# Loads of q and k issued behind GpSimd's regroup, and stores of x one iteration later, in an attention and mixture-of-experts kernel

## The chip, the cores and the metric

The kernel runs on one core of one Trainium2 chip. The core has a matrix engine (PE; PEld is its weight load), a vector engine (DVE), a scalar engine (ACT), GpSimd (POOL) and SyncE (SP), which issues most of the DMAs. All DMAs of the core share 16 DMA engines. The metric is the device time of one execution in microseconds.

## The reference

Attention in chunks of 64 keys, then an expert layer in which every token goes to one of eight experts, then a dense layer with a squared ReLU. All in float32.

```python
# q, k, v: (8, 8, 576, 64); chunk = 64
scores = scale * np.matmul(q_c, k_c.transpose(0, 1, 2, 4, 3))
attn = softmax(scores);  out = np.matmul(attn, v_c)
x = out.transpose(0, 2, 1, 3).reshape(4608, 512)
logits = x @ w_gate;  expert_idx = argmax(logits, axis=1)
out[mask] = gate_w[mask, None] * (np.maximum(x[mask] @ w1[e], 0.0) @ w2[e])   # for each of 8 experts
h = np.maximum(x @ w_in, 0.0);  return h * h @ w_out
```

## The kernel before

Three stages follow each other: `attention()` (0 to about 190 us), `experts()` and `second()`. Only the first is touched, and only it is described here.

**Tiles and units.** The 4608 tokens make 36 tiles of 128 (`NTILE`) and 18 units of two tiles. `load_qk(u)` brings q and k of a unit into one of four buffers (tag `a`), one DMA of 512 KB for each where the unit lies in one batch, two smaller ones where it crosses into the next. So a unit is 1.05 MB. v comes by batches (eight, 1.18 MB each, eight DMAs of 144 KB) from GpSimd's queue, into two buffers. x, the result of a tile, is 0.26 MB; it goes from one of four buffers (tag `x`) to `x_d` in HBM by SP, and PE transposes it from the same buffer for the gate.

**The loop** runs over `it` from -3 to 36. Iteration `it` holds, in this order: GpSimd's regroup of a few halves of units, `scores(it+1)`, `pv(it-1)`, `attn_t(it)`, the transposes of q and k that are four or five halves ahead, the transpose of an older tile's x, and every fourth iteration pieces of the gate: the logits (`gate`), the routing (`gate_t`, `route`), the places (`place`) and GpSimd's scatters of them. In this document tile t stands for what `pv(t)` computes in iteration t+1.

**Halves.** A half z is q (even) or k (odd) of unit z/2. `regroup(z)` (L269) copies it on GpSimd from the unit's buffer into one of four slots of `by_r`; `trans` (L296) transposes it on PE. Unit 0 is transposed straight from its buffer (L279).

**What sets the order.** The program order of each engine is the order in which the code is written. SP's queue holds the loads of q and k (L250), the stores of x (L359) and, from iteration 22, the first loads of the experts' weights (L172). A load of q and k waits until GpSimd has regrouped the unit that held the buffer before; a store waits for DVE's x (L358). What stands behind a waiting instruction on SP waits with it. `load_qk(u+3)` is issued where the last transpose of unit u is written; the store where `pv` has written x. In `pv`, DVE writes x (L358) into a buffer that is free when the store of four tiles before has landed and PE has transposed it; `pv` has one PSUM buffer, so the next tile's `pv` on PE waits for that write.

Of the kernel before, what the change touches and what calls it, by code (L numbers as in the profile page):

```python
# [20 lines left out]
def kernel(ctx, tc, q, k, v, w_gate, w1, w2, w_in, w_out, out):  # L21
    nc = tc.nc
# [7 lines left out]
    NTILE = NT // 128  # L30
    NUNIT = NT // 256
# [31 lines left out]
    x_d = dram.tile([NT, DM], F32, name="x_d")  # L63
# [11 lines left out]
    def tl(tag, shape, dt, name):  # L75
        if tag in fixed:
            ts, n = fixed[tag]
            fixed[tag] = ts, n + 1
            t = ts[n % len(ts)].bitcast(dt)
            k = 1  # L80
            for z in shape[1:]:
                k *= z
            t = t[0:shape[0], 0:k]
            names = "abcde"[:len(shape) - 1]
            return t.rearrange(f"p ({' '.join(names)}) -> p {' '.join(names)}", **dict(zip(names, shape[1:])))
        if tag == "m":

            t = sb.tile([128, 32], F32, tag=tag, name=name, bufs=NBUF[tag]).bitcast(dt)
            names = "abc"[:len(shape) - 1]
            n = 1  # L90
            for z in shape[1:]:
                n *= z
            return t[0:shape[0], 0:n].rearrange(f"p ({' '.join(names)}) -> p {' '.join(names)}", **dict(zip(names, shape[1:])))
        return sb.tile(shape, dt, tag=tag, name=name, bufs=NBUF[tag])
# [134 lines left out]
    def attention():  # L229
        with ExitStack() as actx:  # L230
# [8 lines left out]
            st = {}  # L239

            def load_qk(u):
                qk = tl("a", [128, 2, H, 2 * D], F32, f"qk{u}")
                for j, (src, nm) in enumerate(((q, "q"), (k, "k"))):
                    t = qk[:, j]
                    g = 4 * u
                    done = 0
                    while done < 4:
                        b, c = divmod(g + done, NCB)
                        n = min(4 - done, NCB - c)
                        nc.sync.dma_start(  # L250
                            out=t[32 * done:32 * (done + n)],
                            in_=src[b, :, c * CH:(c + n) * CH, :].rearrange("h (p r) d -> p h (r d)", r=2),
                        )
                        done += n
                    st[nm, u] = t
# [9 lines left out]
            def regroup(z):  # L265
                u, j = divmod(z, 2)
                if u:
                    src = st["qk"[j], u].rearrange("p h (r d) -> p r h d", r=2)
                    nc.gpsimd.tensor_copy(out=by_r[:, z % 4], in_=src)  # L269
# [36 lines left out]
            def scores(i):  # L306
                u, h2 = divmod(i, 2)
                qt, kt = st["qT", u], kb[u % 2]
                ps = ps_s.tile([128, H, CH], F32, tag="s", name="sc")
                for p in range(NPAIR):  # L310
                    for c2 in range(2):
                        c = 2 * h2 + c2
                        nc.tensor.matmul(
                            ps[64 * c2:64 * c2 + 64, 2 * p:2 * p + 2, :],
                            lhsT=qt[:, p, 32 * c:32 * c + 32, :].rearrange("p i r -> p (i r)"),
                            rhs=kt[:, p, c],
                            start=True,
                            stop=True,
                        )
                mx = tl("m", [128, H], F32, "mx")  # L320
                nc.vector.tensor_reduce(mx, ps, axis=AX.X, op=ALU.max)
                at = tl("r", [128, H, CH], F32, "at")
                nc.vector.tensor_tensor(out=at, in0=ps, in1=mx[:, :, None].to_broadcast([128, H, CH]), op=ALU.subtract)
                st["at", i] = at
# [5 lines left out]
            def attn_t(i):  # L330
                at = st.pop(("at", i))
                ps = ps_t.tile([128, NPAIR, 128], F32, tag="t", name="ta")
                for p in range(NPAIR):
                    nc.tensor.transpose(ps[:, p, :], at[:, 2 * p:2 * p + 2, :], ident)
                aT = tl("r", [128, NPAIR, 128], F32, "aT")
                nc.scalar.copy(aT, ps)
                st["aT", i] = aT

            def pv(i):
                aT = st.pop(("aT", i))  # L340
                ps = ps_v.tile([128, 2, 512], F32, tag="v", name="pv")
                for p in range(NPAIR):
                    for c2 in range(2):
                        b, c = divmod(2 * i + c2, NCB)
                        o = (p % 2) * 2 * (D + 1)
                        nc.tensor.matmul(
                            ps[64 * c2:64 * c2 + 64, p // 2, o:o + 2 * (D + 1)],
                            lhsT=aT[:, p, 64 * c2:64 * c2 + 64],
                            rhs=vb[b % 2][p][:, c].rearrange("p j d -> p (j d)"),
                            start=True,  # L350
                            stop=True,
                        )
                pv_ = ps[:, :, 0:4 * (D + 1)].rearrange("p a (h d) -> p a h d", d=D + 1)
                rc = tl("m", [128, 2, 4, 1], F32, "rc")
                nc.vector.tensor_scalar(out=rc, in0=pv_[:, :, :, D:D + 1], scalar1=1e-9, scalar2=None, op0=ALU.add)
                nc.vector.reciprocal(out=rc, in_=rc)
                x = tl("x", [128, 2, 4, D], F32, "x")
                nc.vector.tensor_tensor(out=x, in0=pv_[:, :, :, 0:D], in1=rc.to_broadcast([128, 2, 4, D]), op=ALU.mult)  # L358
                nc.sync.dma_start(out=x_d[128 * i:128 * i + 128, :], in_=x.rearrange("p a h d -> p (a h d)"))  # L359
                st["x", i] = x  # L360

            def get(shape, name):
                return ps_t.tile(shape, F32, tag="t", name=name)
# [39 lines left out]
            def fill_v(s, eng, ps):  # L403
                for t in vb[s][ps]:
                    eng.memset(t[0:64, :, 1, :], 0.0)
                    eng.memset(t[64:128, :, 0, :], 0.0)
                    eng.memset(t[0:64, :, 0, D:D + 1], 1.0)
                    eng.memset(t[64:128, :, 1, D:D + 1], 1.0)
# [37 lines left out]
            regrouped, moved = [0], [0]  # L446

            def trans_upto(z, hh):
                for y in range(moved[0], min(z, NTILE)):
                    u, h2 = divmod(y, 2)  # L450
                    trans("qk"[h2], u, hh)
                    if hh and h2 and u + 3 < NUNIT:
                        load_qk(u + 3)

            for it in range(-3, NTILE + 1):
                ahead_ = it + 4 + (it >= JUMP)
                while regrouped[0] < min(ahead_ + 2, NTILE):
                    regroup(regrouped[0])
                    regrouped[0] += 1
                if it in (-2, 0):  # L460
                    fill_v(1, nc.gpsimd, A if it < 0 else Z)
                if it in (-1, 0):
                    load_v(1, ps=HA if it < 0 else HZ)
                if 0 <= it + 1 < NTILE:
                    scores(it + 1)
                if 0 <= it - 1 < NTILE:
                    pv(it - 1)
                    lo, hi = (2 * (it - 1)) // NCB, (2 * (it - 1) + 2) // NCB
                    if hi > lo and lo + 2 < B:
                        load_v(lo + 2)  # L470
                if 0 <= it < NTILE:
                    attn_t(it)
                if it == JUMP:
                    for hh in range(2):
                        trans_upto(ahead_ - 1, hh)
                    moved[0] = ahead_ - 1
                trans_upto(ahead_, 0)
                for step, i in todo.get(it, ()):
                    step(i, nc.scalar.copy if any(f == gate_route for f, _ in late.get(it, ())) else nc.vector.tensor_copy)
                if 0 <= it + 1 < NTILE:  # L480
                    expo(it + 1)
                trans_upto(ahead_, 1)
                moved[0] = min(ahead_, NTILE)
                if it == 2:
                    constants()
                late_steps(it)
                if it == NTILE - 14:
                    for _ in range(4):
                        load_next(most=1)
                if NTILE - 5 <= it < NTILE - 2:  # L490
                    split(1, 0, it - NTILE + 5, eng=nc.gpsimd)
# [633 lines left out]
```

## Time and profile before

| | |
|---|---|
| median of 3 runs | 1461.23 us (1460.78 to 1465.03) |
| profiled execution, its own time | 1460.37 us |
| its span, first to last instruction | 1458.5 us |
| mean granted TensorE clock | 0.993 |
| PE busy | 1419.3 us, 97% of the span |
| POOL busy | 505.6 us, 35% |

How to read it: PE is busy nearly throughout, so what counts is the time in which it isn't, and the time in which its granted clock is below full. The page's slices are 36 us wide; attention is the first five of them. There PE shows 7 to 9 tenths, GpSimd 5 to 7 and DMA 9 in the first four. From the sixth slice on DMA falls below the full digit and PE stays at 8 and 9.

### The profile page before, as it was taken

How to read it: one execution, taken by the hardware profiler on the slowest of the kernel's cores; microseconds unless marked ns; L12 is line 12 of the kernel's file. 1: busy time of each engine (PE TensorE's matmuls, PEld its weight loads, DVE VectorE, ACT ScalarE, POOL GpSimd, SP SyncE). 2: the span in 40 equal slices, each digit the busy share in tenths (PEclk: the TensorE clock that was granted, in tenths of full speed). 3: DMA queues.
4: the chain of work that ended last, by engine and by line, in shares of the span. 5: the costliest groups of instructions: out<-in, count | busy, mean ns of one | idle time of the engine just before them, and what ended most of it. 6: DMA issues, size and time to landing. Idle time of an engine off the chain costs nothing.

```text
span 1458.5 us, 21568 instructions
## 1 busy us (share of the span) xinstructions
PE 1419.3 (97%) x8186; PEld 1222.9 (84%) x8186; DVE 761.5 (52%) x1371; ACT 549.6 (38%) x936; POOL 505.6 (35%) x608
## 2 busy tenths in 40 slices
PE   7988988999999999999999999999999999999998
PEld 5877788888889999997888888888888888888886
DVE  7767787578888788884432322322332232233222
ACT  4765634444444455554422222222222222222222
POOL 7675755436555446643003040210404012040301
PEclk9999999999999999999999999999999999999999
DMA  9999555767678778885101010100101001010000
GB/s 204 260 259 244 148 162 182 221 192 234 208 225 247 223 234 266 268 257 163 58 15 46 1 60 0 44 17 1 60 0 60 0 26 35 1 60 0 31 2 29
DMA packets 144369, 172.90 MB, mean 119 GB/s; under 512 B 18160, under 2 KB 103872, under 8 KB 144256
## 3 DMA queue, kind: packets, MB, share of 16 engines
q1 hardware_dynamic: 110032, 112.58, 27.0%
q0 software_dynamic: 17920, 40.51, 10.0%
q10 hardware_dynamic: 16304, 18.36, 3.8%
q8 instruction: 65, 1.06, 0.3%
q14 instruction: 48, 0.39, 0.1%
HBM read 133.05 MB, written 38.34 MB: 118 GB/s over the span
## 4 chain that ended last, share of the span: by engine, by line
PE 54%; POOL 0%; POOLq 0%; issue 0%; DVE 0%
PE hp L1034 27%; PE py L1055 27%; POOL out_dram L1015 0%; POOLq L1120 0%; DVE o L1063 0%; POOL between L1014 0%
## 5 line engine op out<-in xcount | busy, mean ns | idle before, releaser
L1034 PE MATMUL hp<-xm,w_None 128*128 128x512 f32 x1728 | 417.5, 391 | 3.3 <-DVEq L978 3.3
L1034 PEld LDWEIGHTS hp<-xm,w_None 128*128 128x128 f32 x1728 | 326.3, 189 | 71.5 <-ACTq L978 3.5
L1055 PE MATMUL py<-w_None,h 128*128 128x512 f32 x1512 | 363.2, 389 | 0.0
L1055 PEld LDWEIGHTS py<-w_None,h 128*128 128x128 f32 x1512 | 283.8, 188 | 58.8
L1039 DVE SCALAR_TENSOR_TENSOR rs<-hp,rs 128x512 f32<-128x512 f32 x144 | 99.5, 691 | 437.7 <-ACT rs L1038 437.7
L1038 ACT ACTIVATE rs<-hp 128x512 f32<-128x512 f32 x144 | 86.0, 597 | 460.0 <-PE hp L1034 460.0
L1015 POOL DMA_INDIRECT out_dram<-o,tp x36 | 35.1, 974 | 630.2 <-ACT o L1061 624.2
L796 PE MATMUL pa<-xs,w 128*128 128x256 f32 (+2 forms) x1344 | 242.3, 329 | 5.7 <-DVE h L800 2.4
L808 PE MATMUL pb<-h,w 128*128 128x256 f32 (+2 forms) x1344 | 243.9, 331 | 0.0
L796 PEld LDWEIGHTS pa<-xs,w 128*128 128x128 f32 x1344 | 211.4, 189 | 23.5 <-DVE h L800 4.8
L808 PEld LDWEIGHTS pb<-h,w 128*128 128x128 f32 x1344 | 209.9, 190 | 14.5
L1041 DVE TENSOR_TENSOR h<-rs,h 128x512 fp32r<-128x512 f32 x144 | 99.7, 692 | 99.0 <-ACT h L1040 99.0
L190 DVE TENSOR_TENSOR w<-raw,w 128x1024 fp32r<-128x1024 f32 x100 | 132.0, 1321 | 17.1 <-ACT w L189 15.3
L799 ACT ACTIVATE h<-pa 128x256 fp32r<-128x256 f32 (+2 forms) x112 | 53.2, 475 | 215.5 <-PE pa L796 185.4
L1040 ACT CAST h<-rs 128x512 fp32r<-128x512 f32 x144 | 89.5, 622 | 110.3 <-DVE rs L1039 110.3
L189 ACT CAST w<-raw 128x1024 fp32r<-128x1024 f32 x113 | 118.1, 1046 | 0.0
L844 POOL TENSOR_TENSOR cr<-cr 128x256 f32<-128x256 f32 x64 | 49.7, 777 | 124.8 <-DVE cr L859 46.6
L800 DVE SCALAR_TENSOR_TENSOR h<-pa,h 128x256 fp32r<-128x256 f32 (+2 forms) x112 | 59.5, 534 | 59.7 <-ACT h L799 55.1
L845 POOL TENSOR_TENSOR cr<-cr 128x256 f32<-128x256 f32 x64 | 73.6, 1149 | 5.0
L223 POOL DMA_INDIRECT xg<-x_d,tk x40 | 44.6, 1115 | 28.1 <-PE pt L785 17.7
L1055 PE MATMUL py<-w,h 128*128 128x512 f32 x216 | 51.7, 389 | 0.0
L210 POOL DMA_INDIRECT tk<-tk_d,at x40 | 41.7, 1042 | 22.1 <-issue 8.5
(204 smaller groups left out, 1325.0 us busy)
## 6 DMA issues: line engine op xcount, KB each, us to landing
raw<-in_moe_w_dram SPq DMA_DIRECT2D x112, 512.0 KB, 4.1
x_d<-x SPq DMA_DIRECT2D x36, 256.0 KB, 6.8
x<-y_d POOLq DMA_DIRECT2D x36, 256.0 KB, 3.0
cr<-in_moe_w_in_dram SPq DMA_DIRECT2D x32, 256.0 KB, 4.2
cr<-in_moe_w_out_dram SPq DMA_DIRECT2D x32, 256.0 KB, 5.5
vb<-in_v_dram POOLq DMA_DIRECT2D x56, 144.0 KB, 8.2
qk<-in_q_dram SPq DMA_DIRECT2D x12, 512.0 KB, 10.1
qk<-in_k_dram SPq DMA_DIRECT2D x12, 512.0 KB, 12.2
```

The source lines that it names most:

```text
L189: nc.scalar.copy(w[0], raw)
L190: eng.tensor_tensor(out=w[1], in0=raw, in1=w[0], op=ALU.subtract)
L796: nc.tensor.matmul(ps[:, 0:N], lhsT=w[wl][:, kk, o:o + 128], rhs=xT[:, xl, kk, 0:N], start=(kk == 0 and wl + xl == 0), stop=(kk == KD - 1 ...
L800: nc.vector.scalar_tensor_tensor(out=h[:, 1, 0:N], in0=ps[:, 0:N], scalar=0.0, in1=h[:, 0, 0:N], op0=ALU.max, op1=ALU.subtract)
L808: nc.tensor.matmul(pb[d][:, 0:N], lhsT=w[wl][:, f % 2, 128 * d:128 * d + 128], rhs=h[:, hl, 0:N], start=(f + hl + wl == 0), stop=(f == NF ...
L845: nc.gpsimd.tensor_tensor(out=af, in0=af, in1=ef, op=ALU.add)
L1034: nc.tensor.matmul(ps, lhsT=w[wl][:, kk, o:o + 128], rhs=xT[:, xl, kk, :], start=(kk == 0 and wl + xl == 0), stop=(kk == KD - 1 and wl == 1))
L1038: nc.scalar.activation(out=rs[:, 0], in_=ps, func=AF.Relu)
L1039: nc.vector.scalar_tensor_tensor(out=rs[:, 1], in0=ps, scalar=0.0, in1=rs[:, 0], op0=ALU.max, op1=ALU.mult)
L1040: nc.scalar.copy(h[:, 0], rs[:, 1])
L1041: nc.vector.tensor_tensor(out=h[:, 1], in0=rs[:, 1], in1=h[:, 0], op=ALU.subtract)
L1055: nc.tensor.matmul(ys[t], lhsT=h[:, hl, 128 * t:128 * t + 128], rhs=w[wl][:, g % 2, :], start=(g == 0 and hl + wl == 0), stop=(g == NF2 - ...
```

## The change

`load_qk` moves from behind the transposes of unit u to right behind GpSimd's regroup of a k half: after the k half of unit w has been written into the program, the load of unit w+3 follows. Unit 3 alone stays where it was, behind the transposes of unit 0. The store of x of the first 24 tiles moves from `pv` into the loop, one iteration later and ahead of that iteration's `pv`; the last 12 stay in `pv`.

```diff
+            def store_x(i):
+                nc.sync.dma_start(out=x_d[128 * i:128 * i + 128, :], in_=st["x", i].rearrange("p a h d -> p (a h d)"))
...
-                nc.sync.dma_start(out=x_d[128 * i:128 * i + 128, :], in_=x.rearrange("p a h d -> p (a h d)"))
                 st["x", i] = x
+                if i >= NTILE - 12:
+                    store_x(i)
...
-                    if hh and h2 and u + 3 < NUNIT:
-                        load_qk(u + 3)
+                    if hh and h2 and u == 0:
+                        load_qk(3)
...
                 while regrouped[0] < min(ahead_ + 2, NTILE):
                     regroup(regrouped[0])
                     regrouped[0] += 1
+                    if regrouped[0] > 2 and regrouped[0] % 2 == 0 and regrouped[0] // 2 + 2 < NUNIT:
+                        load_qk(regrouped[0] // 2 + 2)
...
+                if 0 <= it - 2 < NTILE - 12:
+                    store_x(it - 2)
```

Order on SP near the start, before. The number after `qk` is the unit; L359 is a store of x, tile after tile from tile 0.

```order
L250 DMA qk3_220<-in_q_dram 128x8x128
L250 DMA qk3_220<-in_k_dram 128x8x128
L250 DMA qk4_303<-in_q_dram 64x8x128 x2
L250 DMA qk4_303<-in_k_dram 64x8x128 x2
L359 DMA x_d_63<-x_334 128x512
L359 DMA x_d_63<-x_384 128x512
L250 DMA qk5_409<-in_q_dram 128x8x128
L250 DMA qk5_409<-in_k_dram 128x8x128
L359 DMA x_d_63<-x_446 128x512
L359 DMA x_d_63<-x_503 128x512
L250 DMA qk6_527<-in_q_dram 96x8x128
```

The same place of SP in the changed kernel, where a store of x is L340.

```order
L250 DMA qk4_194<-in_q_dram 64x8x128 x2
L250 DMA qk4_194<-in_k_dram 64x8x128 x2
L250 DMA qk3_225<-in_q_dram 128x8x128
L250 DMA qk3_225<-in_k_dram 128x8x128
L250 DMA qk5_261<-in_q_dram 128x8x128
L250 DMA qk5_261<-in_k_dram 128x8x128
L250 DMA qk6_361<-in_q_dram 96x8x128
L250 DMA qk6_361<-in_q_dram 32x8x128
L250 DMA qk6_361<-in_k_dram 96x8x128
L250 DMA qk6_361<-in_k_dram 32x8x128
L340 DMA x_d_63<-x_337 128x512
L340 DMA x_d_63<-x_392 128x512
```

Units 5 and 6 moved ahead of the first store, and unit 4 moved ahead of unit 3, since the load of unit 3 is still written behind the transposes of that iteration while that of unit 4 is written behind the regroup at its start. GpSimd's own order is unchanged: it regroups unit 3, then 4, then 5.

SP near the end of the loads, before: the stores of tiles 21 to 24 stand among the loads of the experts' weights and of units 16 and 17.

```order
L359 DMA x_d_63<-x_1760 128x512
L172 DMA raw_1798<-in_moe_w1_dram 128x4x256
L172 DMA raw_1800<-in_moe_w1_dram 128x4x256
L172 DMA raw_1802<-in_moe_w1_dram 128x4x256
L172 DMA raw_1804<-in_moe_w2_dram 128x2x512
L359 DMA x_d_63<-x_1832 128x512
L250 DMA qk16_1871<-in_q_dram 128x8x128
L250 DMA qk16_1871<-in_k_dram 128x8x128
L359 DMA x_d_63<-x_1907 128x512
L359 DMA x_d_63<-x_1979 128x512
L250 DMA qk17_2010<-in_q_dram 128x8x128
L250 DMA qk17_2010<-in_k_dram 128x8x128
```

The same in the changed kernel: the first two stores are those of tiles 19 and 20, the last two those of 21 and 22.

```order
L250 DMA qk16_1667<-in_q_dram 128x8x128
L250 DMA qk16_1667<-in_k_dram 128x8x128
L340 DMA x_d_63<-x_1621 128x512
L340 DMA x_d_63<-x_1696 128x512
L172 DMA raw_1800<-in_moe_w1_dram 128x4x256
L172 DMA raw_1802<-in_moe_w1_dram 128x4x256
L172 DMA raw_1804<-in_moe_w1_dram 128x4x256
L172 DMA raw_1806<-in_moe_w2_dram 128x2x512
L250 DMA qk17_1809<-in_q_dram 128x8x128
L250 DMA qk17_1809<-in_k_dram 128x8x128
L340 DMA x_d_63<-x_1763 128x512
L340 DMA x_d_63<-x_1838 128x512
```

Tile 21's store moved behind the four weight loads and unit 17, and tiles 22 to 24 behind unit 17.

## Rows read from the trace of the kernel before

**Rows 1.** Waits of PE, 25 to 145 us: total, times, longest.

```profile
PE tq L296 <- POOL by_r L269: 4.5, 3, 2.5
PE rank L530 <- ACT aT L336: 2.6, 1, 2.6
PE pv L346 <- DVE x L358: 1.1, 1, 1.1
```

**Rows 2.** Timeline of PE (start, length, line, count, idle before); L346 for tiles 6, 8, 10, 21, 26.

```profile
31.73 0.66 PE L296 MATMUL tq<-ident,by_r 128*128 128x128 f32 x4 [0.61 <-POOL by_r L269]
...
46.85 1.06 PE L346 MATMUL pv<-vb,aT 128*64 128x130 f32 x16
...
55.90 1.06 PE L346 MATMUL pv<-vb,aT 128*64 128x130 f32 x16
...
63.90 1.06 PE L346 MATMUL pv<-vb,aT 128*64 128x130 f32 x16
...
77.13 0.66 PE L296 MATMUL tq<-ident,by_r 128*128 128x128 f32 x4 [2.55 <-POOL by_r L269]
...
120.34 2.00 PE L346 MATMUL pv<-vb,aT 128*64 128x130 f32 x16 [1.09 <-DVE x L358]
...
144.01 1.06 PE L346 MATMUL pv<-vb,aT 128*64 128x130 f32 x16
```

**Rows 3.** Timeline of POOL: the copy of half 14, and a run of four copies.

```profile
60.39 1.06 POOL L269 COPY by_r<-qk 128x1024 f32<-128x1024 f32 x1 [6.93 <-DMA qk<-in_q_dram]
...
112.71 3.98 POOL L269 COPY by_r<-qk 128x1024 f32<-128x1024 f32 x4
```

**Rows 4.** Windows: length, five engines' busy, PEclk, DMA share, GB/s (last three columns).

```profile
50.00:110.00 60.00, 56.16 (x675) 48.19 (x668) 41.92 (x107) 39.25 (x72) 42.87 (x59) 0.97 1.10 254
75.00:85.00 10.00, 7.87 (x81) 7.43 (x83) 5.67 (x14) 5.27 (x10) 7.06 (x8) 0.83 1.08 302
115.00:120.00 5.00, 1.66 (x25) 1.23 (x22) 4.65 (x11) 2.33 (x5) 1.73 (x3) 0.91 0.32 99
120.00:125.00 5.00, 4.66 (x29) 4.32 (x30) 3.58 (x10) 2.41 (x5) 2.89 (x5) 0.50 0.76 195
125.00:130.00 5.00, 5.00 (x57) 4.17 (x59) 3.50 (x7) 2.43 (x5) 4.78 (x8) 0.91 1.11 328
```

**Rows 5.** Unit 3's loads (qk, SP, 18.9 to 21.3 us): issue and landing.

```profile
L250 SPq DMA_DIRECT2D qk<-in_k_dram x1: 1632/1632/1632, 19.6 to 19.6; - x1
...
DMA to landing us min/median/max: 13.1/13.1/13.1
```

**Rows 6.** Unit 4's loads (qk, SP, 21.3 to 27.5 us): the later k lands last.

```profile
L250 SPq DMA_DIRECT2D qk<-in_k_dram x2: 1144/1694/2245, 24.0 to 26.3; - x2
...
DMA to landing us min/median/max: 12.1/12.6/13.1
```

**Rows 7.** Unit 7's loads (qk, SP, 45.5 to 48.6 us): q, then k.

```profile
L250 SPq DMA_DIRECT2D qk<-in_k_dram x1: 1980/1980/1980, 46.6 to 46.6; - x1
...
DMA to landing us min/median/max: 14.7/15.0/15.4
```

**Rows 8.** Tile 5's store (x_d, SP, 48 to 53 us), and DVE's wait on stores.

```profile
L359 SPq DMA_DIRECT2D x_d<-x x1: 4660/4660/4660, 48.7 to 48.7; - x1
...
DMA to landing us min/median/max: 13.9/13.9/13.9
...
DVE x L358 <- DMA x_d<-x: 0.4, 1, 0.4
```

**Rows 9.** Unit 17's loads (qk, SP, 142.6 to 144 us): the landing is q's.

```profile
L250 SPq DMA_DIRECT2D qk<-in_q_dram x1: 413/413/413, 142.7 to 142.7; - x1
...
DMA to landing us min/median/max: 5.8/5.8/5.8
```

**Rows 10.** DVE's timeline at 112 us, and all eight L513.

```profile
112.15 4.59 DVE L513 TENSOR_TENSOR lc<-lg,lmx 128x32 f32<-128x32 f32 x1
...
L513 DVE TENSOR_TENSOR lc<-lg,lmx x8: 192/192/4590, 55.7 to 192.7; 128x32 f32<-128x32 f32 x7, 128x64 f32<-128x64 f32 x1
```

## Prediction

> **What bounds the kernel now.** I read the waits of PE first, since PE is busy 97% of the span and the diff touches only the first 190 us. Between 25 and 145 us PE waits 4.5 us in three places for GpSimd's regrouped q and k, and 3.7 us for the routing and for DVE's x [rows 1]. So all that these waits hold is 8.2 us. With them goes clock: PEclk is 0.83 in the 10 us around the second wait for a regroup, and 0.91, 0.50 and 0.91 in the three stretches of 5 us around the routing's wait [rows 4]. At full speed the first would take 1.7 us less (0.17 x 10), the others 3.4 us (0.45 + 2.5 + 0.45). The half-speed stretch has its instruction: 2.00 us for the 16 matmuls of a `pv` that takes 1.06 elsewhere [rows 2]; that is 1.2 instead of 2.4 GHz. What can be gained there is 13.3 us in two lots: 4.5 + 1.7 behind the regroup, 2.6 + 1.1 + 3.4 behind the routing.
>
> Next the reason for the regroup's waits. GpSimd stood 6.93 us until q of unit 7 landed [rows 3], and was late from then on: the 2.55 us wait of PE at 77.13 [rows 2] is for a copy that stood behind v's loads and four scatters in GpSimd's queue. Unit 7's loads took 14.7 and 15.4 us from issue to landing [rows 7]. This is the row that decides what an earlier issue is worth: if the DMA engines were idle ahead of it, an earlier issue is an earlier landing; if they were full, it only changes who waits.
>
> They were full. From 50 to 110 us the 16 engines show a share of 1.10 (packets overlap) and move 254 GB/s [rows 4]. A tile needs 0.52 MB of q and k, 0.26 of v and 0.26 of x, together 1.05 MB, which is 4.13 us at that rate. PE needs (63.90 - 46.85) / 4 = 4.26 us for a tile where it doesn't wait [rows 2]. DMA and PE are level, and the changed order has to be judged by which bytes come first.
>
> **What the change moves.** No byte and no instruction is added. GpSimd's and PE's orders stay; on SP the loads move ahead of two to four stores. In the steady part a load waits for the same regroup as before, and no longer for x of four tiles in between. Three places matter.
>
> *Unit 3 behind unit 4.* Before, unit 3's k was issued at 19.6 and landed 13.1 us later, at 32.7 [rows 5]; unit 4's last part was issued at 26.3 and landed 13.1 us later, at 39.4 [rows 6]. In the new order unit 3 has the later place, so its k lands near 39.4 and its q some 2 us sooner. PE wants q at 31.73, where it already waits 0.61 us [rows 2]. With the copy it will get it near 38: PE is some 6 us late at tile 3. Nothing hides this; unit 4, which is early for it, isn't wanted until later.
>
> *Stores behind loads.* DVE writes x of tile t into the buffer of tile t-4, so the store of t-4 must have landed. The buffer was tight already: the store of tile 5, issued at 48.7 right behind unit 7's loads, landed 13.9 us later at 62.6, and DVE waited 0.4 us for it at tile 9 [rows 8]. In the new order tile 2's store stands right behind unit 7, and those of tiles 3 and 4 behind unit 8. So tile 7's x must wait until unit 8 is in. Count the bytes ahead: units 0 to 8 (9.44 MB), three batches of v (3.54), stores 0 to 3 (1.05): 14.0 MB. By 62.6 us the old order had landed units 0 to 7, the same v and stores 0 to 5: 13.5 MB. The other 0.5 MB is 2.0 us at 254 GB/s: tile 3's store lands at 64.6, tile 7's x is written by 65.3, and `pv` of tile 8 starts near 65.5, where it started at 55.90 [rows 2]. That is 9.6 us late, the first 6 of them included. PE then idles about 4 us in one place; I add 1.7 us for its clock, by the nearest row, the one behind the 2.55 us wait.
>
> *The same chain at the end.* Tile 21's store now stands behind four weight loads and unit 17; tile 25's x waits for it, and `pv` of tile 26 for that. Unit 17's q landed at 142.7 + 5.8 = 148.5 [rows 9] and its k about 1.7 us later, as unit 7's did [rows 7]: 150.2. The new order has three stores fewer ahead (tiles 22 to 24, 0.79 MB, 3.1 us). And the engines no longer fall idle from 115 to 125 us, where SP stood before a store: by the shares 0.32 and 0.76 [rows 4] that is 3.4 + 1.2 = 4.6 us at most, and nothing if the lower share still hides a full queue. So tile 21's store lands between 142.5 and 147.1, and tile 26 can't start before 143.2 to 147.8. Before, it started at 144.01 [rows 2]: -0.8 to +3.8 us, middle +1.5. This is a floor: whatever PE saves before, it gives back here.
>
> *What is saved.* GpSimd gets a unit's data earlier, since the loads have about four tiles (17 us) more; the latter two waits for a regroup and their clock go: 4.5 - 0.6 + 1.7 = 5.6 us.
>
> *The routing's wait.* One L513 of eight on DVE took 4.59 us, the others 0.19 [rows 10]. It began at 112.15 and ended when GpSimd's run of four copies (112.71 to 116.69) ended [rows 3]. PE's 2.6 + 1.1 us and 3.4 us of clock, 7.1 us, hang on it. The run comes about because GpSimd is held by v's loads and the scatters, which stay. The new order makes GpSimd less late against PE by a few us, and a run of four may then meet this routing, another one, or none. I take it as met once, as before; the ends are none (7.1 us less) and two (7.1 us more). The Trainium skill's page "SBUF — State Buffer", section "SBUF: two separate sides", has GpSimd and a DVE instruction with two SBUF inputs exclude each other for one whole instruction; by it alone a meeting would last one copy, about 1 us, where the row shows the whole run of four; by the page the sum would lose most of those 7.1 us and fall to the floor.
>
> **The sum.** 9.6 + 1.7 - 5.6 = +5.7 us at tile 26, above the floor of +1.5. Everything behind tile 26 (the last tiles, experts, second layer) runs on PE in the same order and moves along. On the profiled execution's own 1460.37 us, 0.9 below the median of the runs, this gives 1466.1; I say **1466.0**, 0.33% over the median.
>
> **Rivals.**
>
> *The floor, not slower in a measurable way.* The run of copies meets no routing: 5.7 - 7.1 = -1.4, which lies below the floor, so the floor holds: +1.5, and up to +3 with some clock behind the wait there. For it: the timing moved by several us, and only one L513 of eight met a run. Against it: the pattern of v's loads, scatters and then copies recurs every four or five tiles. Time: 1462 to 1463.5.
>
> *Faster: the engines carry more when SP's queue is never empty.* Between 75 and 85 us they moved 302 GB/s and between 125 and 130 us 328 [rows 4]. At 302 all the way a tile's bytes take 3.5 us, the stores land in time, unit 3's lag shrinks to 1.05 / 0.302 = 3.5 us, and both lots of waits may go: 3.5 - 5.6 - 7.1 = -9.2; with the routing's kept, -2.1. Time: 1451 to 1458. Against it: those stretches are short, and over 60 us with a full share the mean is 254. It decides from a mean of about 268 GB/s: then the bytes of the 114 us between 31 and 145 us pass in 108 (254 x 114 / 108), and the floor falls from +1.5 to -4.5. The same page of the Trainium skill states a DMA peak of about 436 GB/s; an estimate from it is 2.4 us for a tile, by which no store would be late and this rival would win; no row here comes near it.
>
> *The change does nothing.* The loads stand before full DMA engines instead of before x, stores land as late as now, and only neighbours swap: within 1 us, 1460 to 1462.
>
> **How the numbers follow.** Forecast (late start, late stores, one meeting) 0.46; floor 0.34; nothing 0.06; faster 0.14. What a measurement can tell from no change is about 0.3%, 4.4 us. The forecast's case is slower by more than that, the second and third lie within it: faster 0.14, same 0.40, slower 0.46. The range reaches down to 1459.5, which takes in the floor's lower end (1460.4 - 0.8), and leaves out the faster case (0.14). Upward, a second meeting would give 5.7 + 7.1; I take most of it, to 1471.5, and leave out 0.06.
>
> **What would show it.** PE's wait for the regroup of half 6 near 31 us should be 5 to 7 us instead of 0.61; unit 4's loads should stand ahead of unit 3's on SP. DVE should wait for stores of x (0.4 us in all before) by several us near 62 us and again near 145. GpSimd's 6.93 us wait for q of unit 7 should be gone or short. The DMA share should stay above 1 from 110 to 145 us. `pv` of tile 8 should start near 65, of tile 26 near 146 to 150. I am wrong if unit 3's q lands before 34, or if the mean rate over 50 to 110 us rises well above 254 GB/s; then `pv` of tile 26 comes before 143 and the kernel is faster.

## The result, and the profile of the changed kernel

| | before | changed |
|---|---|---|
| median of 6 runs | 1462.45 us (1460.78 to 1465.03) | 1473.05 us (1469.90 to 1475.40) |
| profiled execution, its own time | 1460.37 us | 1474.01 us |
| span | 1458.5 us | 1472.2 us |
| mean granted clock | 0.993 | 0.989 |

The changed kernel is slower: ratio 1.0069, 95% interval 1.0051 to 1.0087. The forecast was 1466.0, its range ended at 1471.5. The sign was right; the size is about twice the forecast (10.6 us between the medians, 5.6 forecast), and the time lies outside the range.

First the waits of PE, 25 to 160 us (total, times, longest), which answer to [rows 1].

```profile
PE pv L349 <- DVE x L361: 9.7, 6, 3.7
PE tq L296 <- POOL by_r L269: 4.8, 1, 4.8
PE rank L538 <- ACT aT L336: 2.3, 2, 1.7
```

And DVE's waits for stores, 20 to 160 us.

```profile
DVE x L361 <- DMA x_d<-x: 11.1, 4, 6.0
```

PE's wait for the regroup is one now and not three; the wait for DVE's x went from 1.1 to 9.7 us, and DVE itself waits 11.1 us for stores where it waited 0.4 [rows 8]. PE's timeline says when. The rows are half 6, then `pv` of tiles 3, 7, 8, 13, 24 and 26 (compare [rows 2]).

```profile
36.08 1.12 PE L296 MATMUL tq<-ident,by_r 128*128 128x128 f32 x4 [4.83 <-POOL by_r L269]
40.60 1.18 PE L349 MATMUL pv<-vb,aT 128*64 128x130 f32 x16
...
63.21 1.11 PE L349 MATMUL pv<-vb,aT 128*64 128x130 f32 x16 [3.75 <-DVE x L361]
69.17 1.06 PE L349 MATMUL pv<-vb,aT 128*64 128x130 f32 x16
...
89.90 1.18 PE L349 MATMUL pv<-vb,aT 128*64 128x130 f32 x16
...
144.50 1.06 PE L349 MATMUL pv<-vb,aT 128*64 128x130 f32 x16
...
156.50 1.11 PE L349 MATMUL pv<-vb,aT 128*64 128x130 f32 x16 [1.33 <-DVE x L361]
```

SP's timeline near the start holds the reason (L250 are loads, L340 stores). Unit 3 is issued at 23.19, right behind unit 4, where it was issued at 18.96. The first two stores go out at 44.46; before, the first went out at 27.55. Tile 3's store goes out at 56.18, behind unit 8.

```profile
23.19 0.55 SPq L250 DMA_DIRECT2D qk<-in_q_dram  x1
23.79 3.82 SPq L250 DMA_DIRECT2D qk<-in_k_dram  x1
27.70 5.03 SPq L250 DMA_DIRECT2D qk<-in_q_dram  x1
32.78 1.81 SPq L250 DMA_DIRECT2D qk<-in_k_dram  x1
41.48 1.87 SPq L250 DMA_DIRECT2D qk<-in_q_dram  x2
43.39 1.03 SPq L250 DMA_DIRECT2D qk<-in_k_dram  x2
44.46 0.92 SPq L340 DMA_DIRECT2D x_d<-x  x2
...
50.65 5.44 SPq L250 DMA_DIRECT2D qk<-in_k_dram  x1
56.18 6.08 SPq L340 DMA_DIRECT2D x_d<-x  x1
```

Two windows (columns as in [rows 4]) show that the DMA engines are less full, not fuller: 226 GB/s instead of 254 from 50 to 110 us, and a hole at 120 us: unit 15's load waits there for a copy of GpSimd's and goes out at 125.05.

```profile
50.00:110.00 60.00, 52.77 (x629) 45.73 (x629) 43.08 (x101) 36.84 (x67) 35.78 (x49) 0.96 0.94 226
120.00:125.00 5.00, 5.00 (x64) 4.16 (x58) 2.49 (x6) 4.23 (x9) 4.35 (x9) 1.00 0.33 62
```

**A ledger.** How late each tile's `pv` starts in the changed kernel, against the kernel before, in two pairs of traces. The first pair is the one above; the second was taken later, both of its traces on one chip (its runs are below).

| `pv` of tile | 3 | 8 | 14 | 24 | 26 | 34 | profiled run |
|---|---|---|---|---|---|---|---|
| forecast, us late | 6 | 11.3 | 5.7 | 5.7 | 5.7 | 5.7 | 5.6 |
| first pair | 6.5 | 13.3 | 8.8 | 8.7 | 12.5 | 13.7 | 13.6 |
| second pair | 5.1 | 11.9 | 6.3 | 5.7 | 10.3 | 11.7 | 13.1 |

Up to tile 24 the forecast is 0 to 3 us off. Between tiles 24 and 26 the pairs lose 3.8 and 4.6 us that it did not have, and the second pair another 2.8 at tile 27.

### The profile page after: what moved, and what is told of

Same layout as the page of the kernel before. It is cut to its first block, busy times and chain, and to the rows that moved or that the text cites. A ratio compares the mean times of both kernels' runs of the same rounds, so it can differ in the third digit from the quotient of the medians.

```text
span 1472.2 us, 21566 instructions
## 1 busy us (share of the span) xinstructions
PE 1424.1 (97%) x8186; PEld 1226.2 (83%) x8186; DVE 765.3 (52%) x1371; ACT 550.0 (37%) x936; POOL 507.1 (34%) x608
## 3 DMA queue, kind: packets, MB, share of 16 engines
q8 instruction: 65, 1.06, 0.3%
## 4 chain that ended last, share of the span: by engine, by line
PE 53%; POOL 0%; POOLq 0%; issue 0%; DVE 0%
PE hp L1042 27%; PE py L1063 26%; POOL out_dram L1023 0%; POOLq L1128 0%; DVE o L1071 0%; POOL between L1022 0%
## 5 line engine op out<-in xcount | busy, mean ns | idle before, releaser
L349 PE MATMUL pv<-vb,aT 128*64 128x130 f32 x576 | 40.7, 285 | 13.4 <-DVE x L361 12.7
L260 POOL DMA_DIRECT2D vb<-in_v_dram x64 | 46.6, 754 | 16.3 <-PE pv L349 16.3
## 6 DMA issues: line engine op xcount, KB each, us to landing
qk<-in_k_dram SPq DMA_DIRECT2D x12, 512.0 KB, 11.3
```

## The experiments

The runs were made on several chips; on some the kernel before itself takes 1470 us instead of 1462. So every ratio is to runs of the kernel before on the same chip.

| kernel | ratio to before | 95% interval |
|---|---|---|
| changed kernel | 1.0069 | 1.0051 to 1.0087 |
| changed, unit 3 first | 1.0051 | 1.0031 to 1.0071 |
| loads only | 1.0042 | 1.0026 to 1.0059 |
| loads only, unit 3 first | 1.0040 | 1.0022 to 1.0058 |
| stores only | 1.0009 | 0.9994 to 1.0023 |
| unit 4 ahead of unit 3 only | 1.0027 | 1.0010 to 1.0043 |
| unit 3 first, eight x buffers | 1.0019 | 1.0004 to 1.0034 |
| changed, ScalarE's stores | 1.0056 | 1.0037 to 1.0076 |
| the same, unit 3 first | 1.0011 | 0.9992 to 1.0030 |
| old loads, ScalarE's stores | 1.0030 | 1.0015 to 1.0045 |
| changed, memset between copies | 1.0067 | 1.0046 to 1.0087 |
| before, memset between copies | 1.0017 | 0.9999 to 1.0035 |
| changed order early only | 1.0043 | 1.0027 to 1.0059 |
| changed order late only | 1.0043 | 1.0027 to 1.0059 |

### The change taken apart

Unit 3 first, the rest as changed:

```diff
                     if hh and h2 and u == 0:
                         load_qk(3)
+                        load_qk(4)
...
-                    if regrouped[0] > 2 and ...
+                    if regrouped[0] > 4 and ...
```

> The changed kernel, with unit 3 loaded ahead of unit 4 again and everything else as it is. Three causes have to be told apart: unit 3 behind unit 4 (tile 3 is 6.5 us late in the changed kernel), stores of x behind the loads (tile 8 is 13.3 us late, so 6.8 more), and something that comes only from the two together. First theory, each cause adds its own part: tile 3 starts as before, near 34; DVE still waits some 4 to 6 us for stores of x between 45 and 70 us; PE does without the 2.55 us wait for a regroup; the time is 6 us under the changed kernel's, 1465 to 1469. Rival, the stores are late only because the loads behind the late unit 3 come in one heap: the waits for stores go as well, and the time is 1456 to 1461, under the kernel before.

Measured 1.0051. Tile 3 starts at 33.80, in time, but tile 5 starts at 49.62, 6.6 us late. DVE's timeline, x of tile 4:

```profile
48.79 0.69 DVE L361 TENSOR_TENSOR x<-pv,rc 128x512 f32<-128x512 f32 x1 [7.84 <-DMA x_d<-x]
```

And PE's, `pv` of tile 5 behind it:

```profile
49.62 2.00 PE L349 MATMUL pv<-vb,aT 128*64 128x130 f32 x16 [6.37 <-DVE x L361]
```

Tile 4 takes the buffer of tile 0, whose store now goes out at 43.61, behind units 5 and 6. In the changed kernel PE waits only 0.81 us here, since it was already 6.5 us late. So the two delays don't add up: the late unit 3 hides most of the first late store. Neither theory had this.

Loads only, with unit 4 ahead and with unit 3 ahead:

```diff
                 st["x", i] = x
-                if i >= NTILE - 12:
-                    store_x(i)
+                store_x(i)
...
-                if 0 <= it - 2 < NTILE - 12:
-                    store_x(it - 2)
```

> Only the loads go out behind the regroup (unit 3 still behind unit 4); stores of x stay where pv writes x. First theory (the parts add): tile 3 is 6.5 us late, no wait for a store of x over 1 us up to tile 12, the 2.55 us wait for a regroup and its clock are gone, so tile 13 is some 2 us late; with the routing's meeting as before 1463 to 1466. Rival (lateness of unit 3 makes all of it): DVE waits for stores here too, and the time is that of the changed kernel, 1471 to 1475.

> Loads behind the regroup from unit 5 on, unit 3 ahead of unit 4, stores of x where pv writes x. First theory: no late tile 3, no late store, and the 4.5 us that an earlier load gave back between tiles 8 and 13 of the changed kernel: 1456 to 1460, under the kernel before. Rival (the DMA engines are full, so an earlier issue only changes who waits): as before, 1461 to 1464, with the 2.55 us wait for a regroup still there or a wait for a store in its place.

The first came nearer the theory than the rival but cost more than the theory had: 1.0042, some 6 us where 2 to 5 were expected; tile 3 is 6.4 us late and tile 13 4.4 instead of 2, and one wait of DVE's for a store is 1.9 us. The second refutes its theory: without the late unit 3 and with the stores in their old place in the code, the earlier loads cost as much, 1.0040. DVE waits 10.7 us for stores in four places, where the kernel before has 0.4. Its timeline at the first three:

```profile
45.53 0.69 DVE L361 TENSOR_TENSOR x<-pv,rc 128x512 f32<-128x512 f32 x1 [4.08 <-DMA x_d<-x]
50.48 0.69 DVE L361 TENSOR_TENSOR x<-pv,rc 128x512 f32<-128x512 f32 x1 [1.96 <-DMA x_d<-x]
62.70 0.69 DVE L361 TENSOR_TENSOR x<-pv,rc 128x512 f32<-128x512 f32 x1 [4.04 <-DMA x_d<-x]
```

A load that goes out sooner stands ahead of a store that was ahead of it, wherever the store is written. That and the late unit 3 are the harm in this change; the store's own move adds little:

```diff
-                    if hh and h2 and u == 0:
-                        load_qk(3)
+                    if hh and h2 and u + 3 < NUNIT:
+                        load_qk(u + 3)
...
-                    if regrouped[0] > 2 and ...
-                        load_qk(regrouped[0] // 2 + 2)
```

> Only the stores of x go out one iteration later, ahead of the next tile's pv; the loads stay behind the transposes of the unit three before, in the old order. First theory: a store one iteration (4.2 us) later with the same loads around it lands 2 to 5 us later in its worst places, and since the buffer was tight (0.4 us in the kernel before) DVE waits 2 to 5 us near tile 9 and 1 to 3 near tile 26: 1465 to 1469. Rival (stores are late only behind the heap of loads): no wait over 1 us, 1461 to 1464.

The rival came closer: 1.0009, no difference that can be measured, though the mechanism is there (DVE waits 2.7 us once, tile 12 is 4.3 us late). At tile 13 it is 0.6 us late: the kernel before waits there anyhow.

The swap alone, the kernel before with `load_qk(4)` issued where `load_qk(3)` stood, and the other way round:

> The kernel before with unit 4 loaded ahead of unit 3 and nothing else changed. Theory now: tile 3 is some 6 us late; DVE waits for no store, since the stores keep their places; up to tile 13 the lateness is paid out of the wait for a regroup that the kernel before has there (4 us), which is the DMA's pace and not the order; so some 2 us are left at tile 13, and what comes on top by tile 30 is the routing's meetings with GpSimd's copies: ratio 1.001 to 1.004. Rival (a late start is never made good): tile 13 and all later ones 6 us late, ratio 1.004 to 1.006.

Measured 1.0027, as the theory had it: tiles 3 to 8 are 6.5 us late, tile 13 3.6, tile 14 3.2. 3.3 us came back with not one load of the steady part issued earlier.

### Taking the late stores away

Eight buffers for x up to tile 17, on top of unit 3 first:

```diff
-                x = tl("x", [128, 2, 4, D], F32, "x")
+                x = tl("q" if i % 2 and i < 18 else "x", [128, 2, 4, D], F32, "x")
```

> The changed kernel with unit 3 first, and with eight buffers for x up to tile 17 (every other tile takes one of the buffers that the experts' weights use later), so that DVE's x of tile t waits for the store of tile t-8. Orders of all queues stay. Theory now, after the run with unit 3 first: a load that goes out earlier stands ahead of stores in SP's queue, the store of tile 0 lands near 48.7, and DVE waits for it at tile 4 (6.4 us of PE), so the four x buffers turn the earlier loads into a loss; unit 3 behind unit 4 only hides the same delay and is no term of its own. Then DVE's wait for stores is under 1 us up to tile 17, tile 8 starts near 56 and tile 13 some 4 us sooner than before, and the time is 6 to 10 us under that of unit 3 first: ratio to the kernel before 0.996 to 0.999. Rival (the engines are full, whoever waits): the wait moves to GpSimd's regroup, PE waits 4 to 8 us for by_r before tile 13, ratio 1.001 to 1.005.

Half right. From 1.0051 it fell to 1.0019, DVE waits for no store before 146 us, and tile 8 starts at 56.33. But tile 13 starts at 81.19, which lies among three traces of the kernel before (80.35, 80.87, 82.75). The window from 30 to 110 us of this kernel:

```profile
30.00:110.00 80.00, 72.29 (x853) 62.02 (x850) 61.77 (x131) 49.50 (x90) 52.00 (x69) 0.98 1.11 251
```

The same of the kernel before:

```profile
30.00:110.00 80.00, 75.49 (x901) 65.03 (x898) 56.39 (x136) 52.73 (x96) 54.02 (x72) 0.98 1.10 254
```

The share is 1.1 and the rate some 250 GB/s in both. With the loads early, unit 3 first and the stores harmless, the same bytes pass at the same rate, and nothing is gained.

The stores of the first 24 tiles from ScalarE, with unit 4 first, with unit 3 first, and with the loads of the kernel before:

```diff
-            def store_x(i):
-                nc.sync.dma_start(
+            def store_x(i, eng=nc.sync):
+                eng.dma_start(
...
-                    store_x(it - 2)
+                    store_x(it - 2, nc.scalar)
```

> The changed kernel (unit 4 ahead of unit 3), with the stores of x of the first 24 tiles issued from ScalarE, so that they stand in another queue than the loads. Theory now (order within SP's queue makes the stores late): a store lands within 2 to 6 us, DVE doesn't wait for any before tile 24, tile 3 is still 6.5 us late and stays so up to tile 12, then 4 us come back where the kernel before waits for a regroup: ratio 1.000 to 1.003. Rival (bytes, not order): stores land some 10 us after their issue from ScalarE too, DVE waits as in the changed kernel, ratio 1.005 to 1.008.

> As the one before with stores from ScalarE, and unit 3 ahead of unit 4. Theory now: neither the late tile 3 nor the late stores, so what unit 3 behind unit 4 costs shows only here, as the difference to the run before: some 4 to 6 us; tile 8 starts at 55 to 57, ratio to the kernel before 0.995 to 0.999. Rival (full engines): the stores' share is taken from the loads, GpSimd waits longer for them and PE waits 4 us or more for by_r before tile 13: ratio 0.999 to 1.003.

> Loads as in the kernel before (behind the transposes of the unit three before); stores of x one iteration later, from ScalarE. SP then holds loads alone, and a load no longer waits behind a store. Theory now: with the stores in another queue the place of the loads in the code matters little, since nothing is left for them to pass: within 0.15% of the run with ScalarE's stores and unit 3 first. Rival (the earlier place behind the regroup is worth something by itself): 3 us or more slower than that run, with PE's 2.5 us wait for by_r near 77 us still there.

DVE waits for no store in any of them (20 to 160 us), so the order in SP's queue did make them late. But none of the three times came as its theory had it. With unit 4 first tile 3 is 10.4 us late and not 6.5, since GpSimd waits 8.63 us for q of unit 3 where it waited 4.36; so the 6.6 us between 1.0056 and 1.0011 are not the price of unit 3's place alone. With the old loads PE waits 3.53 us at 40.36 for half 8, which is q of unit 4 and came late as well, and tile 4 is 3.5 us late. In both, the stores of tiles 0 and 1 go out near 24 and 28 us, beside these loads; in the changed kernel they go out at 44.46. That they take the loads' share, as the second run's rival had it, fits, but was not tested apart. In the run with unit 3 first PE doesn't wait as long for a load, but a store holds ScalarE, and tile 6 is 6.1 us late:

```profile
39.42 0.58 ACT L299 COPY qT<-tq 128x512 f32<-128x512 f32 x1
45.67 0.33 ACTq L340 DMA_DIRECT2D x_d<-x  x1
46.09 0.59 ACT L336 COPY aT<-ta 128x512 f32<-128x512 f32 x1 [6.10 <-DVE at L323]
```

x of that tile was long written; in the program the store's issue also waits until the DMA before it on the same semaphore, a load of SP's (here k of unit 5, issued at 31.1), has landed. What a queue free of such a tie would give was not tried. Their stores took 7.6, 7.6 and 5.9 us from issue to landing in the median, those of the kernel before 7.5 (20 to 150 us): another queue made a store little or no faster. The Trainium skill's page "DMA: Bandwidth & Descriptors", section "Issuing engines are not separate DMA queues", says that DMAs of all issuing engines share the same 16 DMA engines; the trace agrees.

### The routing's meetings

A hold is here what an instruction of the routing on DVE takes beyond its 0.2 us while GpSimd copies. One tiny memset behind each regroup copy, in the changed kernel and in the kernel before:

```diff
                     nc.gpsimd.tensor_copy(out=by_r[:, z % 4], in_=src)
+                    nc.gpsimd.memset(between[0:1, z % 16:z % 16 + 1], 0)
```

> The changed kernel with one tiny memset of GpSimd behind each regroup copy, so that copies of a run don't follow each other directly. In the changed kernel DVE's instructions of the routing that read two SBUF operands are held 9.0 us in all up to 200 us by GpSimd's copies (3.71, 2.53, 2.11 us and smaller), in the kernel before 4.4 us in one place. Theory: DVE gets in only where GpSimd pauses, so a hold shrinks to about one copy, 1.0 us; the sum falls from 9.0 to 3 to 4 us and the ratio from 1.007 to 1.002 to 1.005. Rival one: a hold lasts until the run of copies ends whatever lies between, holds of 2 us and more remain, ratio 1.006 to 1.008. Rival two: holds shrink, but PE's time doesn't hang on them, ratio 1.006 to 1.008.

> The kernel before with the same tiny memset behind each regroup copy. Theory: the one hold of 4.59 us shrinks to about 1 us, and with it PE's 2.6 and 1.1 us and the clock behind them: ratio to the kernel before 0.995 to 0.998. Rival: the hold stays, or the 7 us are lost elsewhere (GpSimd's later copies): 0.999 to 1.001.

Both theories on a gain failed: 1.0067 and 1.0017. In the second, DVE's timeline still shows a hold for a whole run:

```profile
113.99 3.67 DVE L514 TENSOR_TENSOR lc<-lg,lmx 128x32 f32<-128x32 f32 x1
```

GpSimd's timeline beside it:

```profile
114.55 1.04 POOL L269 COPY by_r<-qk 128x1024 f32<-128x1024 f32 x1
115.53 0.09 POOL L270 MEMSET between<- 1x1 int32 x1
115.57 1.03 POOL L269 COPY by_r<-qk 128x1024 f32<-128x1024 f32 x1
```

The memset lies within the copies' ends, so GpSimd didn't pause, and whether a true pause would let DVE in is open. In the changed kernel's run the holds fell from 9.0 to 4.3 us in all and the time stayed: so in this run PE's time didn't hang on their sum. How much of that is chance, a second trace of the kernel before was to show:

> The kernel before once more, for a second trace of it. Its one meeting of the routing with a run of copies (4.4 us of hold), PE's wait of 2.5 us for a regroup near 77 us and tile 13 at 80.9 us are taken as typical: theory, they come again within 0.5 us. Rival: where the routing meets a run is chance, and this trace has none or two.

The rival holds. Tile 13 came at 80.35 and PE's wait there was 2.5 us again, but the holds make 3.0 us with no run of four, and PE waits 5.1 us for a copy near 100 us that the first trace doesn't have:

```profile
99.98 1.12 PE L296 MATMUL tq<-ident,by_r 128*128 128x128 f32 x4 [5.12 <-POOL by_r L269]
```

At tile 34 the two traces of one kernel are 9 us apart. A third trace, below, is 3.6 us behind the first at tiles 10 to 12. So a single pair of traces carries a ledger to about 0.5 us up to tile 9 and to 2 to 4 us up to tile 16; behind that only what recurs counts.

### Where the loss at the end belongs

The changed order up to unit 9 and tile 10 alone, and from there on alone:

```diff
-                if i >= NTILE - 12:
+                if i >= 11:
...
-                    if hh and h2 and u == 0:
-                        load_qk(3)
+                    if hh and h2 and (u == 0 or 10 <= u + 3 < NUNIT):
+                        load_qk(u + 3)
...
-                    if regrouped[0] > 2 and ... < NUNIT:
+                    if regrouped[0] > 2 and ... < 10:
...
-                if 0 <= it - 2 < NTILE - 12:
+                if 0 <= it - 2 < 11:
```

This is the early half. The late half has the complement, with unit 9 issued right behind unit 8.

> The changed order up to unit 9's load and tile 10's store, the order of the kernel before from there on. The changed kernel is 8.7 us late from tile 14 to 16 and again from 22 to 24, and loses 5 more behind tile 24. Theory: lateness once made stays, so this kernel is 7 to 9 us late at tile 14 and about as much at the end, without the 5: ratio 1.004 to 1.006. Rival (the place of the last store is a fixed point in time, up to which lateness is given back): the 8.7 us shrink behind tile 24 to under 3, ratio 1.000 to 1.002.

> The order of the kernel before up to unit 9's load and tile 10's store, the changed order from there on. Theory: the chain of the last loads and stores hangs on GpSimd's copies, which follow PE, so the changed order costs here the 3 to 5 us that the changed kernel loses behind tile 24 although PE isn't late when it gets there: ratio 1.002 to 1.004. Rival one (the prediction's floor): tile 21's store lands at a time that the DMA's pace sets, 142.5 to 147.1, and costs at most 1.5 us in the middle: 0.999 to 1.001. Rival two: those 5 us come of the early lateness and are not there without it: 0.998 to 1.001 as well, but tile 21's store lands before 143.

> The changed kernel once more, for a trace on the same chip as that of the kernel before below. Theory: tile 3 6.5 us late, 4 us lost to stores up to tile 8, 4 us given back at tile 13, as in the first trace within 1 us each. Rival: the pieces behind tile 13 (where the routing meets runs of copies) and those before it change from trace to trace by as much as they are.

> The kernel before once more on the same chip, as the ground for the other three. Theory: as the first two traces up to tile 14 (34.1, 55.9 and 80.9 us for tiles 3, 8 and 13 within 0.6 us); from tile 17 on it lies between them, since there the two differed by 5 us in one wait for a regroup and by the number of the routing's meetings.

The early order alone has the early loss and keeps most of it (1.0043; 7.0 us late at tile 14, 4.9 at 24 against the first trace of before), and near tile 26 DVE waits for no store: tile 26 comes 4.30 us behind tile 25, at PE's own pace. Tile 25 loses 1.7 us here too, so that much at tile 25 doesn't come of the late order. The late order alone is 1.0043 too, but not cleanly: at its seam units 9 and 10 pass stores, and DVE waits 7.86 us at tile 11. Behind tile 24 it loses 2.7 us (6.4 late at tile 24, 9.1 at 26), a little under the theory's 3 to 5; and since the seam has made PE late when it gets there, this run can't tell the late order from lateness. DVE's wait for tile 21's store, in the late order alone:

```profile
152.38 0.69 DVE L361 TENSOR_TENSOR x<-pv,rc 128x512 f32<-128x512 f32 x1 [2.37 <-DMA x_d<-x]
```

In the second trace of the changed kernel:

```profile
154.58 0.69 DVE L361 TENSOR_TENSOR x<-pv,rc 128x512 f32<-128x512 f32 x1 [4.05 <-DMA x_d<-x]
```

And in its first:

```profile
155.75 0.69 DVE L361 TENSOR_TENSOR x<-pv,rc 128x512 f32<-128x512 f32 x1 [2.29 <-DMA x_d<-x]
```

So the wait recurs. Six traces have the late order with the stores on SP, and in all six x of tile 25 waits, 1.8 to 4.0 us (in two the profile names nothing that ended the wait); in the other twelve it doesn't wait. The same six tell a fixed time from one that follows PE:

| trace | `pv` of tile 24 | copy of half 29 ends | x of tile 25 starts |
|---|---|---|---|
| unit 3 first, eight x buffers | 139.30 | 130.79 | 148.59 |
| changed, second trace | 142.08 | 136.36 | 154.58 |
| late order alone | 142.24 | 134.91 | 152.38 |
| changed, first trace | 144.50 | 138.79 | 155.75 |
| unit 3 first | 144.90 | 136.45 | 153.84 |
| changed, memset between copies | 146.51 | 138.10 | 156.34 |

x starts when tile 21's store has landed. That moves by 7.8 us between the traces, always 17.0 to 18.2 us behind the copy. With eight x buffers PE is only 3.5 us late at tile 24 (8.7 in the changed kernel). DVE waits there too, but for a store that lands at 148.5 instead of 155.7:

```profile
148.59 0.69 DVE L361 TENSOR_TENSOR x<-pv,rc 128x512 f32<-128x512 f32 x1 [2.25 <-DMA x_d<-x]
```

The second trace of the changed kernel has the early pieces again within 1.5 us, not within the theory's 1. The third trace of the kernel before lies between the other two at tile 34 (0.9 us behind the first); at tile 13 it came at 82.75, not within 0.6 of 80.9, after a 1.9 us wait for v.

No variant beats the kernel before. The moved stores alone, ScalarE's stores with unit 3 first and the memset in the kernel before can't be told from it.

## Why the prediction was wrong

**Unit 3 behind unit 4: right, in its size partly by luck.** Forecast 6 us, measured 6.5 and 5.1 in the two pairs. PE was to get q near 38 and got it at 36.08, 4.35 us behind 31.73 [rows 2]. The other 2.1 us up to tile 3 are clock, which this term didn't have: four transposes take 1.12 us where they took 0.66, and PEclk is 0.50 (columns as in [rows 4]).

```profile
35.00:40.00 5.00, 3.92 (x24) 3.59 (x26) 0.69 (x1) 1.70 (x3) 1.03 (x1) 0.50 1.11 220
```

**Stores behind loads: right in price, one tile off in place.** Tile 3's store was to land at 64.6 and to hold `pv` of tile 8. It landed 10.1 us after 56.18, at 66.3, but DVE waited only 0.89 us for it. The long wait is one tile sooner, x of tile 6 for tile 2's store behind unit 7:

```profile
62.46 0.69 DVE L361 TENSOR_TENSOR x<-pv,rc 128x512 f32<-128x512 f32 x1 [5.96 <-DMA x_d<-x]
66.35 0.69 DVE L361 TENSOR_TENSOR x<-pv,rc 128x512 f32<-128x512 f32 x1 [0.89 <-DMA x_d<-x]
```

PE's idle at tile 7 is 3.75 us (forecast 4, at tile 8) and tile 8 loses 1.7 us more, as forecast for the clock: PE's operations between the two rows take up to 1.06 us where they take 0.60 at full clock. The forecast saw this place, but not the earlier one, tile 0's store behind units 5 and 6. It adds 1.0 us at tile 5 here and 6.6 when unit 3 comes in time. The forecast gave the landing a time of its own, with the late unit 3 included in it, and here that holds: with unit 3 first tile 3 is in time, and tile 8 still starts at 65.86, where 65.5 was forecast before its clock. The late unit 3 and the late stores are largely alternatives, which is why undoing either gives back little.

**What is saved: the size nearly right by luck, the reason wrong.** Forecast 5.6 us by tile 14; measured 4.5 and 5.6. The prediction credited earlier loads ("about four tiles more"). Measured from the end of the regroup of the k half three units before, behind which the changed kernel writes the load, it went out mostly 3 to 10 us later in the kernel before, and in the changed one at once or, with one exception, up to 5 us later, so far less than 17 us was to be had. And 3 to 4 us come back just as well with old loads: the swap alone goes from 6.5 to 3.2, stores alone from 4.3 to 0.3. It is not a saving. The kernel before stands at tile 13 for bytes that pass at 250 GB/s, and a late PE finds them there. The signal said so: GpSimd's long wait didn't go away, it moved from q of unit 7 [rows 3] to its k.

```profile
62.04 1.04 POOL L269 COPY by_r<-qk 128x1024 f32<-128x1024 f32 x1 [6.69 <-DMA qk<-in_k_dram]
```

**The routing: chance.** "Met once, as before" could not be known. The holds make 4.4, 3.0 and 9.5 us in three traces of the kernel before and 9.0 and 9.7 in two of the changed one; from tile 16 to 24 the lateness changes by -0.2 us in the first pair and -0.6 in the second. So that the term comes to nothing by tile 24 agrees. The second meeting that the range left out, 5.7 + 7.1, would have given 1473.2, which is the measured time by number. The second pair speaks against it as the cause: its holds are alike (9.5 and 9.7), and the changed kernel is 13.1 us slower all the same. In the variants the holds make 3 to 12 us; what sets that was not settled.

**The floor at the end: this is the step that failed.** The prediction gave tile 21's store a landing time of its own, 142.5 to 147.1, worked out from DMA bytes, and took the larger of this floor and of PE's lateness: "whatever PE saves before, it gives back here". But unit 17's load goes out 0.03 us behind the copy of half 29 in all six traces of the table above, and that copy comes in all of them, and in three traces of the kernel before, 0.5 to 3.4 us after `pv` of tile 22 starts, be that at 126.8 or at 135.8. So the chain of loads and stores moves with PE; which of GpSimd's waits ties the copy to PE was not settled (it stands behind four scatters of the routing). In the changed kernel that copy ends at 138.79, unit 17 goes out at 138.82, tile 21's store behind it at 140.81, and the store lands 14.8 us later. GpSimd's copy:

```profile
137.74 1.05 POOL L269 COPY by_r<-qk 128x1024 f32<-128x1024 f32 x1
```

SP's issues behind it:

```profile
138.82 0.37 SPq L250 DMA_DIRECT2D qk<-in_q_dram  x1
139.23 1.48 SPq L250 DMA_DIRECT2D qk<-in_k_dram  x1
140.81 7.65 SPq L340 DMA_DIRECT2D x_d<-x  x3
```

At 155.6 it is 8.5 to 13 us behind the forecast, with PE 8.7 us late at tile 24. The landing itself was not badly worked out for a PE that isn't late: 17.0 to 18.2 us behind the copy of the kernel before, which ends at 127.53, would be 144.5 to 145.8 (an estimate from the table). What failed is that the lateness of 5.7 us was set against this wait, where it moves the wait along. The wait of tile 26 is a term to be added, not a floor. From tile 24 to 26 the two pairs lose 3.8 and 4.6 us, with the stores' 1.3 and 3.1 us of PE's wait in it. The longer one costs clock as well: `pv` of tile 26 runs at half speed, and tile 27 is 13.1 us late. In the second trace:

```profile
155.33 2.00 PE L349 MATMUL pv<-vb,aT 128*64 128x130 f32 x16 [3.09 <-DVE x L361]
```

The rest stands at tile 25: 2.3 us in the first pair, where the routing's holds at 144.7 and 147.1 (2.11 and 0.72 us) are, 1.4 in the second, and 1.7 with the early order alone, which has no such wait. With a term of 4 the forecast would have been 1470; of this the late store's part is 1.3 us in the first pair, and 5.9 with its clock in the second. Not all of the gap is this step: the forecast also stood on an execution of 1460.37, 2.1 us under the median of the kernel before, and by tile 14 the first pair had lost 3.1 us more than forecast, the second 0.6.

**The signal on the DMA share fell with it.** It was to stay above 1 from 110 to 145 us; it was 0.33 from 120 to 125. Taking SP's stores out of the way doesn't keep the engines fed when each load waits for a copy that follows PE.

**Rivals.** "Faster" was refuted by the rate, 226 GB/s from 50 to 110 us instead of the 268 it needed. "The change does nothing" is refuted by the time, 10.6 us between the medians. The floor rival fell with the floor.

## What to carry to other kernels

When loads and stores share an issuing queue, a load issued sooner delays the stores that it passes; ask which buffer waits for each of those stores, before counting what the load gains. Delays at one place are often alternatives and not terms of a sum: undo each alone and both together. A time worked out from bytes is a floor only if nothing in the chain to it starts from the engine whose lateness is in question; otherwise its wait is added to that lateness.

## What the runs showed of the hardware

DVE was held by back-to-back GpSimd copies beyond one copy in most traces (3.71 us under a run of four in the changed kernel, 3.67 with a memset between each two), but in the changed kernel at 144.68 it got in after 2.11 us, while a run of three went on to 147.72. So the hold is neither always one copy nor always the whole run. The Trainium skill's page "SBUF — State Buffer", section "SBUF: two separate sides", has such an exclusion last for one whole instruction; the 3.71 us under copies of 1.0 us each differ from that.

The kernel before took 1462 us on some chips and 1470 on others, and two of its traces were 9 us apart at tile 34, with the same program: a wait of 5.1 us for one copy came in one trace and in no other of that kernel.
